# Where the memory rows' softmax sums stand in a segment's attention stretch, and how its spare work is cut

## The chip, the cores and the metric

One core of one Trainium2 chip runs the whole program. The metric is the device time of one execution in microseconds (us). Engines are named as in the profile: PE (matmul), PEld (weight loads of the same engine), DVE (VectorE), ACT (ScalarE), POOL (GpSimd), SP (a DMA queue).

## The reference

Two kinds of layers alternate, A, B, A, B, on x of 2048 tokens by 512. A is attention with a recurrent memory: 64 segments of 32 tokens, in order, and each needs the 8 memory rows that the one before it gave.

```python
for s in range(n_seg):                      # 64 segments, one after the other
    h = concatenate([mem, xs], axis=1)      # 8 memory rows + 32 tokens
    q, k, v = h @ Wq, h @ Wk, h @ Wv        # 32 heads of 128
    scores = where(mask, q @ k.T * scale, -1e9)
    p = softmax(scores)                     # exp, and its row sum
    o = (p @ v) @ Wo
    mem = o[:, :8]; outs.append(o[:, 8:])
```

B is a gated MLP over all tokens (gelu, a 2048x2048 mixing of tokens, a product). The change concerns A alone: two A layers of 64 segments, 128 in all.

## The kernel before, in words

A segment is computed by `segment(s, ...)` inside `a_block`, with all 32 heads at once, in two halves of 16 heads: r = 0 and r = 1. The order of the instructions on PE, DVE and ACT is the order in which they are written (`tc.manual_schedule`); each engine runs its own list in order. The order of one segment on PE is:

1. The projections (L762): q and k of both halves (`psQ`, `psm`, `psK`), and v of half 0 (`psK`), with the scores of half 0 (`psS`, L1113 and L1117) between.
2. Half of v of half 1 (`psV`, L762), the scores of half 1, and the rest of v of half 1. ACT takes the exponentials (`S`, L1122), DVE multiplies them with the mask (`close`, `E`, L1125).
3. The stretch: `pv(0)` and `pv(1)` (L1162, L1165) multiply the exponentials with the values into `psO[0]` and `psO[1]`. Each of the two is a PSUM tile of two banks; columns 0 to 319 of a bank hold these products. The softmax sums come from matmuls with a matrix of ones: `sums_tokens` (L1154, `psT`) for the tokens' rows; for the memory rows `sums_zero` for half 0 (L1136), which writes into free columns of the score tile `psS` and runs among the matmuls of v, and `sums_one` for half 1 (L1145), into columns 320 to 383 of `psO[1]`, between the token sums and `pv(1)`.
4. The memory rows: `inverse(r)` takes 1/sum on ACT as exp(-ln(sum)) (L1179, then L1180, tile `Rm`), `memory_out(r)` on DVE (L1183) multiplies it with the products into `uT`. The output product of half 0 is `px` (`wo_pairs`, L945), that of half 1 `psO<-Wo` (`wo_rest`, L952). Their sum, turned, is the memory of the next segment (`fold`, `build_hA`, `hT`), without which its projections can't begin.

Work that no segment waits for at once is handed out by `fill()`, which advances a generator by one step: the projections of a later block's tokens (`b_units`, `b_even`, `b_light`) or output products of finished tokens (`y_part`). A quarter is one group of four matmuls in four column groups, 512 columns each. `fill()` is called three times in a segment: ahead of `pv(0)`, ahead of `px`, and behind `wo_rest`. In segments fed by `b_units` and `y_part` the three calls give 1, 2 and 5 quarters (full segments); in those fed by `b_even` and `b_light` 1, 1 and, as a rule, 4 (light segments). Light are segments 0 to 15 and 28 to 59 of the first A layer (of them, 0 has its own order) and 0 to 15 of the second.

`close(r)` is followed on the value side by a copy out of PSUM: `VA` of half 0 on DVE (L1211), of half 1 on ACT (L1226, 512 columns), which stands between the two steps of `inverse(0)`:

```python
            invert = inverse(0, pN.rearrange("p (g q) -> p g q", g=2))
            nc.scalar.copy(VA[:, 1].rearrange("p i e -> p (i e)"), psW[:])
            invert()
            close(1)
```

Of the kernel before, what the change touches and what calls it, by code (L numbers as in the profile page):

```python
# [7 lines left out]
BF16 = mybir.dt.bfloat16  # L8
# [6 lines left out]
P = 128  # L15
# [52 lines left out]
def _consts(ctx, tc, c, b_sp, between):  # L68
    nc = tc.nc
    cp = ctx.enter_context(tc.tile_pool(name="consts", bufs=1))  # L70
    bsp = cp.tile([P, 16], F32, name="bsp")
    tctx = ExitStack()
    tmp = tctx.enter_context(tc.tile_pool(name="consts_tmp", bufs=1))
    maskf = tmp.tile([P, 224], F32, name="maskf")
    nc.gpsimd.memset(maskf[:], 1.0)
    fourth = tmp.tile([P, 4, 32], F32, name="fourth")
    nc.gpsimd.memset(fourth[:], 0.0)
    nc.gpsimd.affine_select(out=fourth[:], in_=fourth[:], compare_op=ALU.not_equal, fill=1.0,
                            base=0, pattern=[[-1, 4], [-4, 32]], channel_multiplier=1)
    own = maskf[:, 160:224].rearrange("p (i q) -> p i q", i=4)  # L80
    is_own = tmp.tile([P, 4, 1], F32, name="is_own")
    nc.vector.tensor_reduce(out=is_own[:], in_=fourth[:], op=ALU.max, axis=mybir.AxisListType.X)
    nc.vector.tensor_copy(own, is_own[:].to_broadcast([P, 4, 16]))
    between()
    for q in range(0, P, 32):
        blk = maskf[q:q + 32, 0:160].rearrange("p (i q) -> p i q", i=4)[:, :, 8:32]
        nc.gpsimd.affine_select(out=blk, in_=blk, compare_op=ALU.is_ge, fill=0.0, base=8,
                                pattern=[[0, 4], [1, 24]], channel_multiplier=-1)
        last = own[q:q + 32, :, 8:16]
        nc.gpsimd.affine_select(out=last, in_=last, compare_op=ALU.is_ge, fill=0.0, base=0,  # L90
                                pattern=[[1, 4], [4, 8]], channel_multiplier=-1)
    maskN = cp.tile([P, 2, 224], BF16, name="maskN")
    nc.vector.memset(maskN[:], 0.0)
    for gs in range(4):
        nc.vector.tensor_copy(maskN[32 * gs:32 * gs + 32, gs % 2, :], maskf[32 * gs:32 * gs + 32, :])
    ones = cp.tile([P, P], BF16, name="ones")
    nc.vector.memset(ones[:], 1.0)
    half = cp.tile([P, 2, 32], BF16, name="half")
    nc.vector.memset(half[:], 0.0)
    for g in range(2):  # L100
        nc.vector.memset(half[64 * g:64 * g + 64, g, :], 1.0)
    bsp_bf = cp.tile([P, 16], BF16, name="bsp_bf")

    def load_bsp():
        nc.vector.memset(bsp_bf[:], 0.0)
        nc.sync.dma_start(bsp_bf[:], b_sp.rearrange("(t p) -> p t", p=P))
        return lambda: nc.vector.tensor_copy(bsp[:], bsp_bf[:])

    c["bsp"], c["load_bsp"] = bsp, load_bsp
    tctx.close()  # L110
    c.update(maskN=maskN, ones=ones, half=half)
    return c


# [603 lines left out]
def a_block(tc, c, rows, front, MV_in, RS_in, MV_out, RS_out, ahead, wo, S, first):  # L718
    nc = tc.nc
    NSEG = S // SEG  # L720
    NB = S // P
    scale = float(DH) ** -0.5
    maskN, ones, half = c["maskN"], c["ones"], c["half"]

    with ExitStack() as ctx:

# [38 lines left out]
        def other_bank(mms, *reads):  # L765

            for m in mms:
                for r in reads:
                    tc.declare_no_dep(m.ins, r.ins, reason="another bank of the tile")
# [48 lines left out]
        def b_units(tb, early=0, alone=False):  # L818
            bs = blk_state[tb]
            order = (0, 2, 1, 3, 4, 5) if early else (4, 5, 0, 2, 1, 3)  # L820

            for k, j in enumerate(order):
                now = k < early
                ps = (accB if k % 2 and not alone and not (now and j == 5) else accA).tile([P, 512], F32, name="psb")[:]
                for kts in (((0,), (1, 2), (3,)), ((0, 1, 2, 3),))[k % 2 or alone]:
                    b_mms(bs, j, ps, kts, now)
                    if kts[-1] != KT - 1:
                        yield

                def out(k=k, j=j, ps=ps, now=now):  # L830
                    b_out(bs, k % 2, j, ps, now, j == (5 if alone else 4))

                if now or k % 2 == 0:
                    copies.append(out)
                else:
                    copies.insert(0, out)
                if now or k % 2 or alone:
                    yield
# [164 lines left out]
        def y_part(G, q, last=False):  # L1003

            for k, _ in enumerate(y_steps(G, q, last)):
                if k in (0, 2):
                    yield
            yield

# [60 lines left out]
        def segment(s, fill, spare1, spare2, spare3, tail, loads):  # L1070
# [4 lines left out]
            VA = vsp.tile([P, 2, 4, DH], BF16, name="VA")  # L1075
# [6 lines left out]
            E = segp.tile([P, 2, 2, 224], BF16, name="E", bufs=1)  # L1082
# [9 lines left out]
            def v_mm(r, ps, kts=range(KT)):  # L1092
                return mm_chunk(ps, lambda kt, cg: hA_cur[:, kt, :], lambda kt, cg: cols_rhs(w, 4 + r, kt, cg), kts)
# [30 lines left out]
            def close(r):  # L1124
                nc.vector.tensor_tensor(out=E[:, r], in0=S[:, r].unsqueeze(1).to_broadcast([P, 2, 224]), in1=maskN[:], op=ALU.mult)  # L1125

            def e_all(e, lo, hi):

                return e[:, :, 0:160].rearrange("p n (i q) -> p n i q", q=40)[:, :, :, lo:hi]

            def e_own(e, b):
                return e[:, :, 160:224].rearrange("p n (i b e) -> p n i b e", i=4, b=2)[:, :, :, b, :]

            def sums_zero(pN):

                return [nc.tensor.matmul(pN[32 * cg:32 * cg + 32, 64 * g:64 * g + 64], lhsT=half[:, g, :], rhs=e_own(E[:, 0], 0) if k else e_all(E[:, 0], 0, 8),  # L1136
                                         start=False, stop=True, tile_position=(0, 32 * cg), skip_group_check=True)
                        for k in range(2) for g in range(2) for cg in range(4)]

            def sums_one():  # L1140

                for k in range(2):
                    for g in range(2):
                        e = E[64 * g:64 * g + 64, 1]
                        nc.tensor.matmul(psO[1][:, g, 320:384], lhsT=ones[64 * g:64 * g + 64, :], rhs=e_own(e, 0) if k else e_all(e, 0, 8),  # L1145
                                         start=(k == 0), stop=True, skip_group_check=True)

            def sums_tokens(ps):

# [7 lines left out]
            def pv(r):  # L1157

                for i in range(4):
                    for g in range(2):  # L1160
                        o = psO[r][:, g, 0:320].rearrange("p (s i q) -> p s i q", s=2, i=4)[:, :, i, :]
                        nc.tensor.matmul(o, lhsT=VA[64 * g:64 * g + 64, r, i, :], rhs=E[64 * g:64 * g + 64, r, :, 40 * i:40 * i + 40],  # L1162
                                         start=(r == 0 and i == 0), stop=True, skip_group_check=True)
                for g in range(2):
                    nc.tensor.matmul(ends(heads40(psO[r][:, g, 0:320])), lhsT=VX[64 * g:64 * g + 64, j4, r, :],  # L1165
                                     rhs=E[64 * g:64 * g + 64, r, :, 160:224], start=False, stop=True, skip_group_check=True)
# [10 lines left out]
            def inverse(r, src):  # L1177
                rm = Rm[:, r]
                nc.scalar.activation(out=rm, in_=src, func=ACT.Ln)  # L1179
                return lambda: nc.scalar.activation(out=rm, in_=rm, func=ACT.Exp, scale=-1.0)  # L1180
# [24 lines left out]
            psS = att.tile([P, 2, 512], F32, name="psS")  # L1205
            scores(0)
            expd = exps(0)
# [8 lines left out]
            psW = accB.tile([P, 512], F32, name="psV")  # L1216
            v_mm(1, psW, (0, 1))
            other_bank(scores(1), expd)
            expd = exps(1)
            v_mm(1, psW, (2,))  # L1220
            pN = psS[:, 0, 224:352]
            other_bank(sums_zero(pN), expd)
            v_mm(1, psW, (3,))
            Rm = segp.tile([P, 2, 2, 64], F32, name="Rm", bufs=1)
            invert = inverse(0, pN.rearrange("p (g q) -> p g q", g=2))
            nc.scalar.copy(VA[:, 1].rearrange("p i e -> p (i e)"), psW[:])  # L1226
            invert()
            close(1)

            psO = [attO[r].tile([P, 2, 512], F32, name="psO") for r in range(2)]  # L1230
            if not begin:
                fill()
            pv(0)
            psT = att.tile([P, 2, 512], F32, name="psT")
            sums_tokens(psT)
            sums_one()
            pv(1)
            memory_out(0)
            spare1(E)
            if not begin:  # L1240
                fill()
            inverse(1, psO[1][:, :, 320:384])()
            memory_out(1)
            run(copies)
            Rt = segp.tile([P, 2, 512], F32, name="Rt", tag="Rt", bufs=1)
# [247 lines left out]
```

## Time and profile before

| | us |
|---|---|
| median of three runs | 1604.93 (1603.9 to 1605.56) |
| the profiled execution, its own time | 1610.6 |
| its span in the trace | 1608.9 |
| PE busy | 1579.1 (98%) |
| DVE busy | 1070.4 (67%) |
| ACT busy | 1052.3 (65%) |
| POOL busy | 306.5 (19%) |

Times within the trace are microseconds from the start of the span. A line of the timeline shows the start, the length, the engine, the line of the code, the operation, the tiles (written <- read), how many instructions it takes together, and in brackets how long the engine had been idle and what ended that. A row of matmuls lasts from the first start to the last end. In the chain of waits a piece lasts from the end of the piece before it to its own end.

### The profile page before, as it was taken

The numbers are of one execution on the slowest core, as the hardware profiler recorded it, in microseconds if no ns is written. First come the engines' busy times: TensorE is split into PE (matmuls) and PEld (weight loads), VectorE is DVE, ScalarE is ACT, GpSimd is POOL, SyncE is SP. The second block draws the span as 40 slices with busy tenths as digits, with TensorE's granted clock in tenths as the row PEclk, the third lists the DMA queues.
The fourth block names the chain that finished last, engine by engine and source line by source line (L and its number), as shares of the span: only waits on it lengthen the run. The fifth ranks groups of instructions, "written<-read, shape, count | busy, mean of one in ns | idle before, by whom it ended". The sixth has DMA issues, their size and how long they took to land.

```text
span 1608.9 us, 90911 instructions
## 1 busy us (share of the span) xinstructions
PE 1579.1 (98%) x41021; PEld 981.3 (61%) x41046; DVE 1070.4 (67%) x3066; ACT 1052.3 (65%) x2279; POOL 306.5 (19%) x674
## 2 busy tenths in 40 slices
PE   7899999999999999999999999999999999999999
PEld 3566666666666666666656666666666766665565
DVE  4667766677777776784466666666677667768622
ACT  4677777777777777670057777777777777776400
POOL 6211111112211221320011111111122122224000
PEclk9999999999999999999999999999999999999999
DMA  9322112222311332378952212212233223426698
GB/s 364 131 57 46 40 44 44 50 42 82 80 43 40 87 86 61 106 172 175 209 162 45 48 44 50 44 47 46 73 92 73 47 72 92 97 54 178 143 194 164
DMA packets 255773, 149.67 MB, mean 93 GB/s; under 512 B 188504, under 2 KB 231104, under 8 KB 255384
## 3 DMA queue, kind: packets, MB, share of 16 engines
q1 hardware_dynamic: 241464, 97.68, 27.4%
q0 software_dynamic: 13920, 46.18, 8.9%
q8 instruction: 321, 5.26, 1.4%
q14 instruction: 68, 0.56, 0.1%
HBM read 60.21 MB, written 39.55 MB: 62 GB/s over the span
## 4 chain that ended last, share of the span: by engine, by line
PE 92%; DMA 5%; issue 1%; DVE 1%; ACT 1%; POOL 1%; SPq 0%; POOLq 0%; DVEq 0%; ACTq 0%
PE psQ L762 13%; PE psK L762 13%; PE psb L762 9%; PE pg L403 9%; PE psO L952 7%; PE px L945 7%; PE psm L762 7%; PE psV L762 7%; PE pwB L964 3%; PE psO L1162 3%; PE pz L302 3%; PE py L446 2%; PE psT L1154 2%; PE psS L1113 2%; DMA Wk_sb<-in_A_Wk_dram 1%
## 5 line engine op out<-in xcount | busy, mean ns | idle before, releaser
L762 PEld LDWEIGHTS <-hT 128*32 128x32 bf16 x12288 | 345.3, 96 | 259.2 <-DVE hT L1062 17.7
L762 PE MATMUL psV<-Wv_sb,hT 128*32 128x512 bf16 x2048 | 166.4, 379 | 0.0
L1087 ACT CAST rows<-psQ 128x512 bf16<-128x512 f32 x256 | 145.4, 588 | 23.2 <-PE psQ L762 19.4
L1183 DVE TENSOR_TENSOR uT<-psO,Rm 128x128 bf16<-128x128 f32 x256 | 74.6, 291 | 123.6 <-ACT Rm L1180 123.4
L1090 DVE STREAM_TRANSPOSE QQ<-rows 128x256 f32<-128x256 f32 x256 | 112.5, 439 | 66.2 <-ACT rows L1087 63.6
L1122 ACT ACTIVATE S<-psS 128x224 bf16<-128x224 f32 x256 | 92.2, 360 | 98.1 <-PE psS L1117 98.1
L1090 DVE STREAM_TRANSPOSE KA<-rows 128x256 f32<-128x256 f32 x256 | 113.0, 441 | 64.9 <-ACT rows L1087 62.4
L403 PE MATMUL pg<-z,wspT 128*128 128x344 bf16 x1024 | 154.3, 309 | 0.0
L762 PE MATMUL psK<-Wv_sb,hT 128*32 128x512 bf16 x2048 | 153.2, 378 | 0.0
L1186 DVE TENSOR_TENSOR uT<-psO,Rt 128x384 bf16<-128x384 f32 x256 | 139.9, 547 | 16.4 <-ACT Rt L1265 14.4
L1265 ACT ACTIVATE Rt<-Rt 128x512 f32<-128x512 f32 x256 | 147.3, 622 | 4.0
L952 PE MATMUL psO<-Wo_high,uT 128*32 128x128 bf16 x8192 | 143.0, 219 | 4.1 <-issue 2.2
L762 PE MATMUL psQ<-Wq_sb,hT 128*32 128x512 bf16 x2048 | 136.4, 379 | 0.2 <-issue 0.2
L762 PE MATMUL psQ<-Wk_sb,hT 128*32 128x512 bf16 x2048 | 136.2, 379 | 0.0
L762 PE MATMUL psK<-Wk_sb,hT 128*32 128x512 bf16 x2048 | 136.0, 379 | 0.0
L762 PE MATMUL psm<-Wq_sb,hT 128*32 128x512 bf16 x2048 | 136.0, 379 | 0.0
L945 PE MATMUL px<-Wo,uT 128*32 128x256 bf16 x3840 | 133.8, 273 | 1.3 <-issue 1.2
L952 PEld LDWEIGHTS <-uT 128*32 128x32 bf16 x8192 | 123.6, 97 | 16.2 <-issue 7.8
L403 PEld LDWEIGHTS <-wspT 128*128 128x128 bf16 x1024 | 100.1, 98 | 53.4 <-issue 0.4
L1262 ACT ACTIVATE Rt<-psT 128x1024 f32<-128x1024 f32 x127 | 130.1, 1024 | 3.1
L945 PEld LDWEIGHTS <-uT 128*32 128x32 bf16 x4096 | 104.5, 97 | 25.2 <-issue 2.6
L1044 POOL COPY KX<-old 128x128 bf16<-128x128 bf16 x128 | 65.5, 539 | 263.8 <-PE psS L1117 170.7
(224 smaller groups left out, 2892.9 us busy)
## 6 DMA issues: line engine op xcount, KB each, us to landing
o_d<-o_sb SPq DMA_DIRECT2D x126, 64.0 KB
vb_d<-front SPq DMA_DIRECT2D x31, 256.0 KB
VX<-vb_d SPq DMA_DIRECT2D x124, 64.0 KB
ln_x<-xd SPq DMA_DIRECT2D x26, 256.0 KB
y_o<-o_d POOLq DMA_DIRECT2D x22, 256.0 KB, 3.4
xd<-y_o POOLq DMA_DIRECT2D x22, 256.0 KB, 3.2
Wq_sb<-in_A_Wq_dram POOLq DMA_DIRECT2D x8, 512.0 KB, 7.1
Wk_sb<-in_A_Wk_dram POOLq DMA_DIRECT2D x8, 512.0 KB, 9.3
```

Of the source, the lines that this page charges most:

```text
L403: nc.tensor.matmul(pg[t][:, k, 0:344], lhsT=wsp[t][:, st, :], rhs=z(st, 344 * k, 344 * k + 344), start=(st == 0), stop=(st == NT - 1))
L762: return [nc.tensor.matmul(ps[32 * cg:32 * cg + 32, :], lhsT=lhs(kt, cg), rhs=rhs(kt, cg), start=(kt == 0), stop=(kt == KT - 1), tile_posi ...
L945: nc.tensor.matmul(px[at:at + 32, 0:256], lhsT=lhs[:, h, :], rhs=wo_rhs(h, slice(k + 2, None, -2) if h % 2 else slice(k, None, 2)), start= ...
L952: nc.tensor.matmul(pw[32 * cg:32 * cg + 32, :], lhsT=lhs[:, h, :], rhs=wo_rhs(h, cg), start=False, stop=(h == H - 1), tile_position=(0, 32 ...
L1044: eng.tensor_copy(KX[r][:].rearrange("p g (k i) -> p i g k", i=4), bs["KTB"][:, r].rearrange("p (i g) k -> p i g k", i=4)[:, :, :, 8 * j4: ...
L1087: return r, mms, copy(r[:].rearrange("p (n el two) -> p n el two", n=8, two=2), ps.rearrange("p (n two el) -> p n el two", n=8, two=2))
L1090: nc.vector.transpose(out=(QQ[:, j % 2, :, 0:32] if j < 2 else KA[:, j % 2]).bitcast(F32).rearrange("p n q one -> p n (q one)"), in_=r[:]. ...
L1122: return nc.scalar.activation(out=S[:, r], in_=psS[:, r, 0:224], func=ACT.Exp, scale=scale)
L1183: nc.vector.tensor_tensor(out=hview(uT_cur[:], r, 24, 32), in0=oview(r, 0, 8), in1=Rm[:, r].rearrange("p g (n q) -> p g n q", q=8), op=ALU ...
L1186: nc.vector.tensor_tensor(out=hview(uT_nxt[:], r, 0, 24), in0=oview(r, 8, 32), in1=rview(r, 0, 24), op=ALU.mult)
L1262: nc.scalar.activation(out=Rt[:], in_=psT[:], func=ACT.Ln)
L1265: nc.scalar.activation(out=rt, in_=rt, func=ACT.Exp, scale=-1.0)
```

## The change

- `sums_zero` and the constant `half` go. A new `sums_memory` makes the memory sums of both halves with four matmuls each, as `sums_one` did for half 1.
- The banks are exchanged: the sums of half 0 are put into columns 320 to 383 of `psO[1]`, those of half 1 into the same columns of `psO[0]`.
- The order in the stretch becomes: fill, sums of half 0, `pv(0)`, sums of half 1, token sums, `pv(1)`, `memory_out(0)`, fill, `inverse(1)`, `memory_out(1)`. Both steps of `inverse(0)` are issued behind the sums of half 0.
- The value copy of half 1 is made in two pieces of 256 columns, one on ACT, one on DVE.
- The steps of `b_units` and `y_part` are cut so that the three calls of `fill()` give 2, 1 and 5 quarters in full segments. `b_even` and `b_light` are as they were.

```diff
@@ b_units
-                for kts in (((0,), (1, 2), (3,)), ((0, 1, 2, 3),))[k % 2 or alone]:
+                for kts in (((0, 1), (2,), (3,)), ((0, 1, 2, 3),))[k % 2 or alone]:
@@ y_part
-                if k in (0, 2):
+                if k in (1, 2):
                     yield
@@ segment
-            def sums_zero(pN):
-
-                return [nc.tensor.matmul(pN[32 * cg:32 * cg + 32, 64 * g:64 * g + 64], lhsT=half[:, g, :], rhs=e_own(E[:, 0], 0) if k else e_all(E[:, 0], 0, 8),
-                                         start=False, stop=True, tile_position=(0, 32 * cg), skip_group_check=True)
-                        for k in range(2) for g in range(2) for cg in range(4)]
-
-            def sums_one():
+            def sums_memory(r, ps, begun):
 
                 for k in range(2):
                     for g in range(2):
-                        e = E[64 * g:64 * g + 64, 1]
-                        nc.tensor.matmul(psO[1][:, g, 320:384], lhsT=ones[64 * g:64 * g + 64, :], rhs=e_own(e, 0) if k else e_all(e, 0, 8),
-                                         start=(k == 0), stop=True, skip_group_check=True)
+                        e = E[64 * g:64 * g + 64, r]
+                        nc.tensor.matmul(ps[:, g, :], lhsT=ones[64 * g:64 * g + 64, :], rhs=e_own(e, 0) if k else e_all(e, 0, 8),
+                                         start=(k == 0 and not begun), stop=True, skip_group_check=True)
@@
-            v_mm(1, psW, (2,))
-            pN = psS[:, 0, 224:352]
-            other_bank(sums_zero(pN), expd)
-            v_mm(1, psW, (3,))
+            v_mm(1, psW, (2, 3))
+            close(1)
+            for k, copy in enumerate((nc.scalar.copy, nc.vector.tensor_copy)):
+                copy(VA[:, 1, 2 * k:2 * k + 2].rearrange("p i e -> p (i e)"), psW[:, 256 * k:256 * k + 256])
             Rm = segp.tile([P, 2, 2, 64], F32, name="Rm", bufs=1)
-            invert = inverse(0, pN.rearrange("p (g q) -> p g q", g=2))
-            nc.scalar.copy(VA[:, 1].rearrange("p i e -> p (i e)"), psW[:])
-            invert()
-            close(1)
 
             psO = [attO[r].tile([P, 2, 512], F32, name="psO") for r in range(2)]
             if not begin:
                 fill()
+            sums = [psO[1 - r][:, :, 320:384] for r in range(2)]
+            sums_memory(0, sums[0], False)
+            inverse(0, sums[0])()
             pv(0)
+            sums_memory(1, sums[1], True)
             psT = att.tile([P, 2, 512], F32, name="psT")
             sums_tokens(psT)
-            sums_one()
             pv(1)
             memory_out(0)
             spare1(E)
             if not begin:
                 fill()
-            inverse(1, psO[1][:, :, 320:384])()
+            inverse(1, sums[1])()
             memory_out(1)
```

More of the change, by code (lines that the diff above doesn't have):

```diff
@@ L97, in _consts @@
     nc.vector.memset(ones[:], 1.0)
[L98 to L101, printed above, removed]
     bsp_bf = cp.tile([P, 16], BF16, name="bsp_bf")
@@ L110, in _consts @@
     tctx.close()
-    c.update(maskN=maskN, ones=ones, half=half)
+    c.update(maskN=maskN, ones=ones)
     return c
@@ L722, in a_block @@
     scale = float(DH) ** -0.5
-    maskN, ones, half = c["maskN"], c["ones"], c["half"]
+    maskN, ones = c["maskN"], c["ones"]
     with ExitStack() as ctx:
```

## The prediction

> **What bounds the kernel now.** I read the page first, then the chain of waits over one segment, then the timeline of the same stretch, then the list of waits.
>
> ```profile
> span 1608.9 us, 90911 instructions
> ...
> PE 1579.1 (98%) x41021; PEld 981.3 (61%) x41046; DVE 1070.4 (67%) x3066; ACT 1052.3 (65%) x2279; POOL 306.5 (19%) x674
> ...
> PE 92%; DMA 5%; issue 1%; DVE 1%; ACT 1%; POOL 1%; SPq 0%; POOLq 0%; DVEq 0%; ACTq 0%
> ```
>
> PE is nearly never idle and carries 92% of the chain: now each piece of PE's work costs its own length, and any wait put on PE costs its own length too. The chain of waits through one full segment (segment 25 of the first A layer; start, length, piece):
>
> ```profile
> 295.37 0.22 PE psV L762 x4
> 295.59 0.12 PE psS L1136 x16
> 295.70 0.22 PE psV L762 x4
> 295.92 0.22 PE psb L762 x4
> 296.14 0.25 PE psO L1162 x8
> 296.39 0.06 PE psO L1165 x2
> 296.44 0.30 PE psT L1154 x4
> 296.74 0.06 PE psO L1145 x4
> 296.80 0.14 PE psO L1162 x8
> 296.95 0.06 PE psO L1165 x2
> 297.00 0.55 PE psb L762 x8
> 297.55 0.87 PE px L945 x32
> 298.42 0.89 PE psO L952 x64
> ```
>
> There is PE alone in it, without a gap. A quarter costs 0.22; the first piece behind a change between the column form of the projections and the 64-row form of the stretch has some 0.11 on top (0.25 against 0.14 for the same eight matmuls; 0.55 for two quarters). `sums_zero` costs 0.12, the four-matmul form 0.06. The timeline of the same stretch shows what runs beside it:
>
> ```profile
> 295.12 0.68 DVE L1211 CAST VA<-psK 128x512 bf16<-128x512 f32 x1
> 295.46 0.36 ACT L1122 ACTIVATE S<-psS 128x224 bf16<-128x224 f32 x1 [0.75 <-PE psS L1117]
> 295.85 0.39 DVE L1125 TENSOR_TENSOR E<-S,maskN 128x448 bf16<-128x448 bf16 x1
> 295.97 0.58 ACT L1226 CAST VA<-psV 128x512 bf16<-128x512 f32 x1
> 296.07 0.32 PE L1162 MATMUL psO<-E,VA 64*128 64x80 bf16 x8
> 296.45 0.31 ACT L1180 ACTIVATE Rm<-Rm 128x128 f32<-128x128 f32 x1
> 296.58 0.22 PE L1145 MATMUL psO<-E,ones 64*128 64x64 bf16 x4
> 296.78 0.22 PE L1165 MATMUL psO<-E,VX 64*128 64x128 bf16 x2
> 296.80 0.29 DVE L1183 TENSOR_TENSOR uT<-psO,Rm 128x128 bf16<-128x128 f32 x1 [0.56 <-ACT Rm L1180]
> 297.04 0.28 ACT L1179 ACTIVATE Rm<-psO 128x128 f32<-128x128 f32 x1 [0.28 <-PE psO L1165]
> 297.35 0.31 ACT L1180 ACTIVATE Rm<-Rm 128x128 f32<-128x128 f32 x1
> 297.37 1.04 PE L945 MATMUL px<-Wo,uT 128*32 128x256 bf16 x30
> 297.69 0.29 DVE L1183 TENSOR_TENSOR uT<-psO,Rm 128x128 bf16<-128x128 f32 x1 [0.27 <-ACT Rm L1180]
> 298.25 1.07 PE L952 MATMUL psO<-Wo_high,uT 128*32 128x128 bf16 x64
> ```
>
> I count from S, the start of the second exponential (295.46), since all of the change lies behind it. `memory_out(0)` ends at 296.80 + 0.29, S + 1.63, and `px` starts at S + 1.91; `memory_out(1)` ends at 297.69 + 0.29, S + 2.52, and `wo_rest` (psO L952) starts at S + 2.79. So both memory products are ready some 0.27 before PE needs them: slack, and the change spends it. A light segment (30) shows how much slack there is without the second quarter ahead of `px`:
>
> ```profile
> 345.17 0.36 ACT L1122 ACTIVATE S<-psS 128x224 bf16<-128x224 f32 x1 [0.75 <-PE psS L1117]
> 345.79 0.32 PE L1162 MATMUL psO<-E,VA 64*128 64x80 bf16 x8
> 346.51 0.29 DVE L1183 TENSOR_TENSOR uT<-psO,Rm 128x128 bf16<-128x128 f32 x1 [0.56 <-ACT Rm L1180]
> 346.65 0.40 PE L964 MATMUL pwB<-Wo_high,front 128*32 128x512 bf16 x4
> 346.88 1.04 PE L945 MATMUL px<-Wo,uT 128*32 128x256 bf16 x30
> 347.41 0.29 DVE L1183 TENSOR_TENSOR uT<-psO,Rm 128x128 bf16<-128x128 f32 x1 [0.61 <-ACT Rm L1180]
> 347.76 1.08 PE L952 MATMUL psO<-Wo_high,uT 128*32 128x128 bf16 x64
> ```
>
> None: `memory_out(1)` ends at 347.41 + 0.29 = 347.70, and `wo_rest` starts 0.06 later. That 0.06 is the handoff from DVE to a started matmul. Here `px` starts at S + 1.71, `wo_rest` at S + 2.59.
>
> **The change part by part.**
>
> *The sums of half 0.* Sixteen matmuls (0.12) become four (0.06): PE gains 0.06 a segment. No change of form is added, because the new four stand ahead of `pv(0)` in its form and take over the 0.11 that `pv(0)` pays now. The matrix `half` costs three memsets fewer, once: nothing. But the sums come later. `pv(0)` starts at S + 0.61 in the full segment and at S + 0.62 in the light one. Without the 0.12, and with one more quarter (0.22) in the full segment alone, the new sums start at S + 0.71 and S + 0.50. Four of them last 0.22 (row L1145): they end at S + 0.93 and S + 0.72. ACT begins 0.04 after a matmul's end (296.78 + 0.22 to 297.04).
>
> *From the sums to `px`.* The rows of half 1 give the length of ln, exp and product without a break: 297.04 to 297.98, 0.94. So `memory_out(0)` ends at S + 0.93 + 0.04 + 0.94 = 1.91 (full) and 0.72 + 0.04 + 0.94 = 1.70 (light), and `px` starts 0.06 later: S + 1.97 and S + 1.76. What PE could do: from `pv(0)` to `px` it needs now 1.30 (full: 1.91 - 0.61) and 1.09 (light: 1.71 - 0.62). Behind the change there are 0.06 of sums more and, in the full segment, one quarter less: it is there at S + 0.71 + 1.30 + 0.06 - 0.22 = 1.85, and at S + 0.50 + 1.09 + 0.06 = 1.65. It waits 0.12 and 0.11, and `px` is 0.06 and 0.05 later than now.
>
> *From `memory_out(0)` to `wo_rest`.* Here lies the larger cost. The sums of half 1 are now in `psO[0]`, which `memory_out(0)` reads on DVE. In the list of waits ln of half 1 now waits for `pv(1)`:
>
> ```profile
> ACT Rm L1179 <- PE psO L1165: 38.8, 128, 1.9
> ```
>
> Its own sums (296.58 + 0.22 = 296.80) were ready 0.24 before it started; it waited for the last other instruction on the same tile, 128 times of 128. So a reader of `psO` is ordered behind what stands before it on that tile, whichever columns those touch. In the instructions of the changed kernel, in their built order, ln of half 1 carries one wait, on DVE, for `memory_out(0)` of its own segment; the wait for `pv(1)` is gone from it. The Trainium skill ("PSUM — Partial Sum Buffer", section on bank collisions) says that two engines may not touch one bank and quadrant at once, "reads against reads included", and that PSUM is guarded by bank and not by address: by that rule this wait has to be there. Without it the sum would be that of the second rival below. The price of the wait: from DVE's end to ACT's start it is 0.03 (741.29 + 0.18 to 741.50):
>
> ```profile
> 741.29 0.18 DVE L146 BATCH_NORM_AGGREGATE MV<-bnst 128x2 f32<-128x6 f32 x1
> 741.50 0.29 ACT L122 ACTIVATE RS<-MV,eps_t 128x1 f32<-128x1 f32 x1 [19.33 <-DVE MV L146]
> ```
>
> So ln of half 1 starts at S + 1.94 and 1.73, `memory_out(1)` ends 0.94 later, S + 2.88 and 2.67, and `wo_rest` starts 0.06 later: S + 2.94 and S + 2.73. Now they are 2.79 and 2.59. That is 0.15 and 0.14 a segment. Queued behind the waiting ln on ACT are exp, the copies that are due and the `cross` copy of `px`, which ends later than ln and exp anyway; behind `memory_out(1)` on DVE is the fold, which waits for `px` in any case.
>
> *The value copy in two pieces.* Not in the trace. ACT takes 0.28 for 128 columns (L1179) and 0.58 for 512, so some 0.38 for 256; DVE 0.29 (L1183) and 0.68 (L1211), so some 0.42. psV is ready 0.12 earlier: ACT's piece runs from S + 0.39 to 0.77, ln of half 0 in the light segment (S + 0.76) just about fits. In the built order DVE's piece waits for ACT's, so it runs from S + 0.80 to 1.22, and the second half of `pv(1)` may start at S + 1.28. PE is there at S + 0.71 + 0.06 + 0.20 + 0.06 + 0.30 + 0.07 = 1.40 (full) and 1.19 (light): 0.09 of waiting, which the 0.11 before `px` swallows. I take nothing for it. At the lower bound, 0.28 and 0.29, that also holds; at the upper, 0.58 and 0.68, PE comes late to `px` by about 0.2 in every segment: the third rival. `pv(1)` also waits for ln of half 0 (S + 0.97 + 0.28, full), and the second sums for `close(1)` (S + 0.78): both within 0.1 of PE's own time and under the same cover.
>
> *The quarters.* In full segments one quarter moves from between `pv(1)` and `px` to ahead of the sums, without which the sums would be 0.22 sooner, but PE 0.22 nearer to `px` too. It is paid for already above. Behind `wo_rest` five stay, so the way from `wo_rest` over the fold and the turned memory to the next projections is as it is.
>
> *Sum.* 64 full segments at 0.15 and 63 light ones at 0.14 (segment 0 of the first layer is bound by loads and left out): 9.6 + 8.8 = 18.4 us, on the profiled execution's own 1610.6: 1629.0. The median lies 5.7 below that execution, and I carry that over: 1604.9 + 18.4 = 1623.3. Put otherwise: PE saves 0.06 and gets 0.12 of waiting before `px` and 0.1 before `wo_rest`. Error of the steps: 0.03 on the four handoffs and the start after a wait makes 4 to 5 us either way, so 1618 to 1629.
>
> **The rivals.**
>
> *Work sets the end (faster).* If ln, exp and product came through in time, PE's 0.06 less would be all: 127 x 0.06 = 7.6, 1597.3. For that `memory_out(0)` has to end at S + 1.79 in place of 1.91, and ln of half 1 must not be held by it. For it speaks PE's share of the chain, against it that all three durations repeat in both segments shown. Chance 0.06.
>
> *One wait only.* If ln of half 1 is not held by `memory_out(0)`, `wo_rest` follows `px` directly (0.88 behind it, as now): 0.06 and 0.05 a segment, 7.0 us, 1612. The row of L1179 speaks against it. Chance 0.08. Between this and the first rival lies what can't be told from no change (0.2%, 3.2 us).
>
> *The copies bind.* If the halved copies take nearly what the whole ones take, `pv(1)` is late and with it `px`: about 0.2 in each of 127 segments on top where they are at the upper bound, 25 us, 1649; halfway, 1636. It decides from the point where DVE's piece ends after S + 1.25 in light and 1.35 in full segments. Chance 0.11.
>
> **How the numbers follow.** Forecast 1623, chance 0.75, own range 1618 to 1629. For 8 in 10 the range reaches down to the second rival's side, 1613, and up toward the third, 1632. Slower by over 0.2% are the forecast, the third rival and most of the second: 0.91; faster 0.06; within 0.2% 0.03.
>
> **What would show it.** In the changed profile: ln of half 1 idle until DVE's `memory_out(0)`, in nearly all 128 segments; PE's weight loads of `px` and of `wo_rest` waiting for `uT`; `px` at about S + 1.97 and S + 1.76, `wo_rest` 0.97 behind it; PE busy less by some 0.2 a segment while the span grows. I am wrong if `wo_rest` follows `px` at 0.88, if `px` starts before S + 1.91 in full segments, or if `pv(1)` waits for the copies so long that `px` is late by it.

## The result and the profile after

The changed kernel took 1621.85 us (median of 4 runs, 1618.62 to 1622.56), the kernel before 1604.74 (median of 4, 1603.9 to 1605.56) beside it: ratio 1.0103, 95% interval 1.0089 to 1.0118. It is slower by 17.1 us. The forecast was 1623.0, range 1613 to 1632. The two profiled executions lie only 8.0 us apart (spans 1608.9 and 1616.9); why the medians differ more is taken up at the end.

The page of the changed kernel, span and busy times:

```profile
span 1616.9 us, 87837 instructions
...
PE 1595.1 (99%) x39510; PEld 944.1 (58%) x39510; DVE 1126.3 (70%) x3191; ACT 1050.7 (65%) x2279; POOL 305.6 (19%) x674
```

PE is busy for 16.0 us more, though the page counts 1511 matmuls fewer. The forecast had it less busy. Half of the 16.0 us is the longer span (8.0 us), the other half idle time of PE, which shrank from 29.8 to 21.8 us. A look at one segment says why a PE that waits counts as busy. The timeline of full segment 98 of the changed kernel (counted through both A layers, so segment 34 of the second; lines are shifted: ln is L1169, exp L1170, `memory_out` L1173, `px` L941, `wo_rest` L948, the value copy L1213, the memory sums L1135; S is 1172.43):

```profile
1172.43 0.36 ACT L1118 ACTIVATE S<-psS 128x224 bf16<-128x224 f32 x1 [0.75 <-PE psS L1113]
...
1172.82 0.37 ACT L1213 CAST VA<-psV 128x256 bf16<-128x256 f32 x1
...
1173.13 0.23 PE L1135 MATMUL psO<-E,ones 64*128 64x64 bf16 x4
...
1173.22 0.42 DVE L1213 CAST VA<-psV 128x256 bf16<-128x256 f32 x1
...
1173.41 0.28 ACT L1169 ACTIVATE Rm<-psO 128x128 f32<-128x128 f32 x1 [0.21 <-PE psO L1135]
...
1174.06 0.29 DVE L1173 TENSOR_TENSOR uT<-psO,Rm 128x128 bf16<-128x128 f32 x1 [0.41 <-ACT Rm L1170]
...
1174.38 0.28 ACT L1169 ACTIVATE Rm<-psO 128x128 f32<-128x128 f32 x1 [0.36 <-DVE uT L1173]
1174.40 0.78 PEld L941 LDWEIGHTS <-uT 128*32 128x32 bf16 x32 [0.26 <-DVE uT L1173]
...
1175.03 0.29 DVE L1173 TENSOR_TENSOR uT<-psO,Rm 128x128 bf16<-128x128 f32 x1 [0.35 <-ACT Rm L1170]
...
1175.38 0.68 PEld L948 LDWEIGHTS <-uT 128*32 128x32 bf16 x48 [0.20 <-DVE uT L1173]
```

Read the brackets downward. ln of half 0 begins 0.05 after its sums (1173.13 + 0.23). `memory_out(0)` ends at 1174.35; ACT, idle for 0.36, is released by it (`<-DVE uT L1173`) and begins ln of half 1 at 1174.38; the weight loads of `px` are released by the same product at 1174.40. `memory_out(1)` ends at 1175.32 and releases `wo_rest` at 1175.38. So `px` stands at S + 1.97 and `wo_rest` 0.98 behind it.

A light segment (30) of the changed kernel, S = 346.35, with the fold of `px` (tile `t`) and the first quarter behind `wo_rest`:

```profile
346.35 0.36 ACT L1118 ACTIVATE S<-psS 128x224 bf16<-128x224 f32 x1 [0.75 <-PE psS L1113]
...
348.10 0.28 ACT L1169 ACTIVATE Rm<-psO 128x128 f32<-128x128 f32 x1 [0.36 <-DVE uT L1173]
...
348.12 1.05 PE L941 MATMUL px<-Wo,uT 128*32 128x256 bf16 x30
...
349.09 0.90 PEld L948 LDWEIGHTS <-uT 128*32 128x32 bf16 x64 [0.20 <-DVE uT L1173]
...
349.61 0.29 DVE L1051 TENSOR_TENSOR t<-px,cross 128x128 f32<-128x128 f32 x1
...
350.00 0.39 PE L758 MATMUL psb<-Wq_sb,hB 128*32 128x512 bf16 x4
```

`px` at S + 1.77, `wo_rest` 0.97 behind it, again through DVE's product. The last two rows are for later: the quarter begins 0.91 behind `wo_rest`.

The list of waits of the changed kernel says that these two segments stand for all (engine, line and what it waited for; us in total, times, longest):

```profile
ACT Rm L1169 <- DVE uT L1173: 47.6, 128, 2.0
...
PEld L948 <- DVE uT L1173: 24.3, 122, 0.2
...
PEld L941 <- DVE uT L1173: 18.9, 79, 0.3
```

ln of half 1 waits for `memory_out(0)` 128 times of 128, and the weight loads of both output products wait for `uT` (`px` 79 times, `wo_rest` 122 times), 43.2 us together. That is idle time of the weight loads, not loss of the same size: in segment 98 those of `wo_rest` idle for 0.20, and `wo_rest` is 0.10 later against `px` than before. In the trace of before, the weight loads of `px` waited 0.7 us for `uT` in all. These waits stand on the rows of the weight loads, not of the matmuls: a matmul's row runs on to its modelled end, which covers a wait of 0.1, so PE's busy time grows although its work shrinks. In the segments that simply repeat, PE's rows show no gap in either kernel (worked out from the traces).

### The profile page after: what moved, and what is told of

It reads as the page before. It is cut to its first block, busy times and chain, and to the rows that moved or that the text cites. A ratio compares the mean times of both kernels' runs of the same rounds, so it can differ in the third digit from the quotient of the medians.

```text
span 1616.9 us, 87837 instructions
## 1 busy us (share of the span) xinstructions
PE 1595.1 (99%) x39510; PEld 944.1 (58%) x39510; DVE 1126.3 (70%) x3191; ACT 1050.7 (65%) x2279; POOL 305.6 (19%) x674
## 4 chain that ended last, share of the span: by engine, by line
PE 93%; DMA 3%; DVE 1%; issue 1%; ACT 1%; POOL 0%; POOLq 0%; SPq 0%; DVEq 0%; ACTq 0%
PE psQ L758 13%; PE psK L758 13%; PE psb L758 10%; PE pg L399 9%; PE px L941 8%; PE psO L948 8%; PE psm L758 7%; PE psV L758 7%; PE pwB L960 3%; PE pz L298 3%; PE py L442 2%; PE psO L1152 2%; PE psT L1144 2%; PE psO L1135 2%; PE psS L1109 2%
## 5 line engine op out<-in xcount | busy, mean ns | idle before, releaser
L758 PEld LDWEIGHTS <-hT 128*32 128x32 bf16 x12288 | 315.1, 97 | 274.5 <-DVE hT L1058 22.0
L758 PE MATMUL psV<-Wv_sb,hT 128*32 128x512 bf16 x2048 | 150.3, 378 | 0.0
L1176 DVE TENSOR_TENSOR uT<-psO,Rt 128x384 bf16<-128x384 f32 x256 | 140.2, 548 | 10.9 <-ACT Rt L1254 1.2
L1173 DVE TENSOR_TENSOR uT<-psO,Rm 128x128 bf16<-128x128 f32 x256 | 74.7, 292 | 98.1 <-ACT Rm L1170 96.8
L948 PE MATMUL psO<-Wo_high,uT 128*32 128x128 bf16 x8192 | 139.3, 220 | 0.5 <-issue 0.3
L941 PE MATMUL px<-Wo,uT 128*32 128x256 bf16 x3840 | 135.5, 275 | 0.4 <-issue 0.3
L948 PEld LDWEIGHTS <-uT 128*32 128x32 bf16 x8192 | 116.5, 97 | 26.3 <-DVE uT L1173 24.3
L941 PEld LDWEIGHTS <-uT 128*32 128x32 bf16 x4096 | 99.2, 97 | 28.2 <-DVE uT L1173 18.9
```

The lines of the kernel that those rows point to most:

```text
L758: return [nc.tensor.matmul(ps[32 * cg:32 * cg + 32, :], lhsT=lhs(kt, cg), rhs=rhs(kt, cg), start=(kt == 0), stop=(kt == KT - 1), tile_posi ...
L941: nc.tensor.matmul(px[at:at + 32, 0:256], lhsT=lhs[:, h, :], rhs=wo_rhs(h, slice(k + 2, None, -2) if h % 2 else slice(k, None, 2)), start= ...
L948: nc.tensor.matmul(pw[32 * cg:32 * cg + 32, :], lhsT=lhs[:, h, :], rhs=wo_rhs(h, cg), start=False, stop=(h == H - 1), tile_position=(0, 32 ...
L1173: nc.vector.tensor_tensor(out=hview(uT_cur[:], r, 24, 32), in0=oview(r, 0, 8), in1=Rm[:, r].rearrange("p g (n q) -> p g n q", q=8), op=ALU ...
L1176: nc.vector.tensor_tensor(out=hview(uT_nxt[:], r, 0, 24), in0=oview(r, 8, 32), in1=rview(r, 0, 24), op=ALU.mult)
```

## Experiments

Each ratio is to the kernel before on the same chip. Periods (start of the `psQ` projections to the next such start, in segments without a stall) are worked out from the traces: before 10.03 in full and 9.67 in light segments, changed 10.21 and 9.78. That is 64 x 0.18 + 63 x 0.11 = 18.4 us. Not every segment repeats so. Some take longer than the rest of their kind, which is called a stall here: of the 62 full and 63 light periods within the two layers, 32 and 30 lie within 0.03 of the given figure before, and 52 and 33 in the changed kernel. Nearly all others are longer; they are taken up at e11.

**e1, e3: the sums back in one bank pair.** Both sums go into `psO[1]`, side by side; e3 also puts the quarters back (the edit of e2).

```diff
-            sums = [psO[1 - r][:, :, 320:384] for r in range(2)]
+            sums = [psO[1][:, :, 320 + 64 * r:384 + 64 * r] for r in range(2)]
...
-            pw = psO[1][:, 0, 384:512]
+            pw = psO[0][:, 0, 384:512]
```

> The changed kernel, but the sums of half 1 go into columns 384 to 447 of psO[1], beside those of half 0, and the output product psO<-Wo into psO[0]. In the built order ln of half 1 then waits for pv(1) on PE and no longer for memory_out(0) on DVE. Theory A (two waits: the first puts px 0.06 later, the second, ln of half 1 behind memory_out(0), puts wo_rest another 0.10 later): the second goes, wo_rest follows px at 0.87 to 0.88 in place of 0.976, px stays at S + 1.98 and S + 1.765; 0.06 a segment remain against before, 1612 us (1610 to 1614). Theory B (the bank costs nothing; the two-piece copy, the later sums and the order of the quarters cost all of it): 1622 as the changed kernel.

> Both edits together: sums of half 1 in psO[1], quarters 1, 2 and 5. Theory A: full segments as with the quarters alone (px at S + 1.94, wo_rest 0.88 behind it), light segments as with the bank alone (px S + 1.765, wo_rest 0.88 behind it): 0.03 a full and 0.05 a light segment over before, 1610 us (1607 to 1612). Theory B: 1622 or more.

Measured: e1 1637.52 us, 1.0165 [1.0146, 1.0185]; e3 1636.84 us, 1.0161 [1.0142, 1.0179]. In e1 both theories missed. e3 is slow, as theory B said, but for a cause that neither theory names. e1, full segment 98:

```profile
1184.73 0.36 ACT L1118 ACTIVATE S<-psS 128x224 bf16<-128x224 f32 x1 [0.75 <-PE psS L1113]
...
1185.71 0.28 ACT L1169 ACTIVATE Rm<-psO 128x128 f32<-128x128 f32 x1 [0.21 <-PE psO L1135]
...
1186.04 0.23 PE L1135 MATMUL psO<-E,ones 64*128 64x64 bf16 x4 [0.17 <-ACT Rm L1169]
...
1186.90 1.04 PE L941 MATMUL px<-Wo,uT 128*32 128x256 bf16 x30
...
1187.77 0.46 PE L948 MATMUL psO<-Wo_high,uT 128*32 128x128 bf16 x20
```

The wait for `memory_out(0)` is gone, as expected: `wo_rest` is 0.87 behind `px`. But `px` is at S + 2.17. The sums of half 1 (1186.04) now write the tile that ln of half 0 is reading (1185.71 + 0.28 = 1185.99), in other columns, and they wait for it. That is PE itself, and all behind it is late. The list of waits of e1:

```profile
PE psO L1135 <- ACT Rm L1169: 21.3, 124, 0.2
```

124 times (e3: 126 times, 21.7 us). The exchange thus has a use: with the sums of half 1 ahead of the token sums, one bank pair would cost more than the exchange does.

**e6: one bank pair, the sums of half 1 behind the token sums.** The second edit lets ln of half 0 end before PE gets to the sums.

```diff
-            sums = [psO[1 - r][:, :, 320:384] for r in range(2)]
+            sums = [psO[1][:, :, 320 + 64 * r:384 + 64 * r] for r in range(2)]
...
-            sums_memory(1, sums[1], True)
             psT = att.tile([P, 2, 512], F32, name="psT")
             sums_tokens(psT)
+            sums_memory(1, sums[1], True)
...
-            pw = psO[1][:, 0, 384:512]
+            pw = psO[0][:, 0, 384:512]
```

> The changed kernel with the sums of half 1 in psO[1] beside those of half 0 (the product psO<-Wo in psO[0]), and these sums made behind the token sums. In the run with the bank alone PE itself waited, because the sums of half 1 write the tile that ln of half 0 is reading; behind the token sums that ln has just ended. Theory A: px stays at S + 1.98 and S + 1.765, wo_rest follows at 0.873 in place of 0.976: 0.063 a full and 0.055 a light segment over before, 7.5 us, ratio 1.0047. Theory B (the bank costs nothing): 1.0103 or more.

Measured: 1612.29 us, 1.0022 [1.0007, 1.0037]. Full segment 98 of e6:

```profile
1170.43 0.36 ACT L1118 ACTIVATE S<-psS 128x224 bf16<-128x224 f32 x1 [0.75 <-PE psS L1113]
...
1172.22 0.28 ACT L1169 ACTIVATE Rm<-psO 128x128 f32<-128x128 f32 x1 [0.18 <-PE psO L1155]
...
1172.42 1.05 PE L941 MATMUL px<-Wo,uT 128*32 128x256 bf16 x30
...
1173.30 0.62 PE L948 MATMUL psO<-Wo_high,uT 128*32 128x128 bf16 x32
```

ln of half 1 is released by `pv(1)` (L1155), no longer by DVE; `px` is at S + 1.99 and `wo_rest` 0.88 behind it. The first wait is all that is left: periods 10.11 and 9.75. This is the state that the rival "One wait only" described. So in the changed kernel the exchange of banks costs 0.10 a full and 0.03 a light segment, and the other 0.08 arises ahead of `px`. By its segments e6 should lose 127 x 0.08 = 10.2 us, and it lost 3.2 (interval 1.1 to 6.0); e1, by 10.30 and 9.93, should lose 33.7 and lost 25.8. What takes back 7 to 8 us is not in the segments without a stall; I come back to it at e11.

**e5: the exchange alone, in the kernel before.** The sums of half 1 go into `psO[0]`, where they stood otherwise.

```diff
-                        nc.tensor.matmul(psO[1][:, g, 320:384], lhsT=ones[64 * g:64 * g + 64, :], rhs=e_own(e, 0) if k else e_all(e, 0, 8),
-                                         start=(k == 0), stop=True, skip_group_check=True)
+                        nc.tensor.matmul(psO[0][:, g, 320:384], lhsT=ones[64 * g:64 * g + 64, :], rhs=e_own(e, 0) if k else e_all(e, 0, 8),
+                                         start=False, stop=True, skip_group_check=True)
...
-                                         start=(r == 0 and i == 0), stop=True, skip_group_check=True)
+                                         start=(i == 0), stop=True, skip_group_check=True)
...
-            inverse(1, psO[1][:, :, 320:384])()
+            inverse(1, psO[0][:, :, 320:384])()
```

> The kernel before with the exchange of banks alone: the sums of half 1 go to columns 320 to 383 of psO[0], those of half 0 stay early, in the score tile; in the built order ln of half 1 then waits for memory_out(0). Theory A (the wait costs only what exceeds the slack): ln of half 1 moves from S + 1.585 to S + 1.66 and memory_out(1) ends at S + 2.60; full segments have slack to S + 2.73 and lose nothing, light ones lose 0.08 before wo_rest and get about half of it back behind it, where they now wait 0.04 for the fold: 1 to 3 us, ratio 1.0012. Theory B (the exchange costs 0.1 in every segment): 12 us, ratio 1.008.

Measured: 1619.38 us, 1.0072 [1.0049, 1.0094]. Full segments keep 10.03, as theory A said; light ones lose 0.15, which it did not (63 x 0.15 = 9.4 us; measured 10.3). Light segment 30 of e5:

```profile
346.70 0.36 ACT L1122 ACTIVATE S<-psS 128x224 bf16<-128x224 f32 x1 [0.75 <-PE psS L1117]
...
347.82 0.22 PE L1145 MATMUL psO<-E,ones 64*128 64x64 bf16 x4
...
348.16 0.29 DVE L1183 TENSOR_TENSOR uT<-psO,Rm 128x128 bf16<-128x128 f32 x1 [0.68 <-PE psO L1145]
...
348.50 1.05 PE L945 MATMUL px<-Wo,uT 128*32 128x256 bf16 x30
```

`memory_out(0)` itself now waits for the sums of half 1 (347.82 + 0.22 = 348.04), the last to write its tile, and begins at S + 1.46, where it began at 1.34 before (346.51 - 345.17). `px` is 0.09 later (S + 1.80 against 1.71), and ln of half 1 is chained behind it too. Full segments have the second quarter as cover.

**e2: the quarters as before (1, 2, 5) in the changed kernel. e8: the quarters alone (2, 1, 5) in the kernel before.** The edit of e2; e8 is its reverse.

```diff
-                for kts in (((0, 1), (2,), (3,)), ((0, 1, 2, 3),))[k % 2 or alone]:
+                for kts in (((0,), (1, 2), (3,)), ((0, 1, 2, 3),))[k % 2 or alone]:
...
-                if k in (1, 2):
+                if k in (0, 2):
```

> The changed kernel with the steps of b_units and y_part as before the change: 1, 2 and 5 quarters in full segments; light segments unchanged. Theory A: the sums of full segments come 0.22 sooner, so px is no longer held by memory_out(0) but by PE's own work, at about S + 1.94; ln of half 1 ends early enough and wo_rest follows px at 0.88, S + 2.82 in place of 2.95. 0.14 less in each of 64 full segments: 1613 us (1611 to 1616); light segments as in the changed kernel. Theory B (the quarter ahead of the stretch covers the late copy and is needed): pv(1) waits for the copy, px is at S + 2.0 or later, 1622 or more.

> The kernel before with the quarters of full segments at 2, 1 and 5, and nothing else. Theory A: the sums of half 0 stay early, so px is where it was (S + 1.91); pv(1) and with it ln of half 1 are 0.22 later, memory_out(1) ends at S + 2.74 and wo_rest starts at S + 2.80, 0.01 later than before: 0 to 1 us, ratio 1.0005. If the quarter ahead of the stretch costs by itself what the changed kernel showed for it (0.13 in each full segment): 8 us, ratio 1.005.

Measured: e2 1616.72 us, 1.0035 [1.0021, 1.0048]; e8 1610.31 us, 1.0013 [0.9998, 1.0028]. Full segment 98 of e2:

```profile
1169.83 0.36 ACT L1118 ACTIVATE S<-psS 128x224 bf16<-128x224 f32 x1 [0.75 <-PE psS L1113]
...
1170.22 0.39 DVE L1121 TENSOR_TENSOR E<-S,maskN 128x448 bf16<-128x448 bf16 x1
...
1170.63 0.42 DVE L1213 CAST VA<-psV 128x256 bf16<-128x256 f32 x1
1170.66 0.23 PE L1135 MATMUL psO<-E,ones 64*128 64x64 bf16 x4
...
1170.99 0.36 PE L1152 MATMUL psO<-E,VA 64*128 64x80 bf16 x8
...
1171.78 1.04 PE L941 MATMUL px<-Wo,uT 128*32 128x256 bf16 x30
...
1172.66 0.68 PE L948 MATMUL psO<-Wo_high,uT 128*32 128x128 bf16 x36
```

Full segment 98 of e8:

```profile
1161.31 0.36 ACT L1122 ACTIVATE S<-psS 128x224 bf16<-128x224 f32 x1 [0.75 <-PE psS L1117]
...
1163.19 1.04 PE L945 MATMUL px<-Wo,uT 128*32 128x256 bf16 x30
```

In e8 `px` is at S + 1.88, no later than before, and nothing is lost: early sums in `psS` do not mind a quarter behind them. In e2 `px` is at S + 1.95 and `wo_rest` 0.88 behind it, so PE waits for neither product; full segments take 10.07, light ones 9.78 as in the changed kernel. The quarter ahead costs 0.14 a full segment, but only together with the late sums.

10.07 is still 0.04 more than before, though PE has less to do. The rows show two smaller waits that the quarter had covered: the sums of half 1 begin 0.05 after the mask product of half 1 has ended (1170.22 + 0.39 to 1170.66), and `pv(1)` takes 0.36, where segment 98 of the changed kernel has 0.32; it needs DVE's piece of the copy, which ends at 1171.05. In the chain of waits of this segment the four sums take 0.14 in place of 0.06, and the eight matmuls of `pv(1)` 0.18 in place of 0.14. Theory B of e2 was thus right in kind, but not in size.

**e10: one bank pair, the order of e6, the quarters of e2.**

> The changed kernel with three things at once: both memory sums in the second bank pair, those of half 1 behind the token sums, and the quarters as before (1, 2, 5). Theory A (two waits, one of which the quarter ahead of the sums makes in full segments): neither wait is left in full segments: px where PE arrives, S + 1.95 as with the quarters put back, wo_rest 0.88 behind, period 10.07; light segments as with that order alone, 9.75. By the segments 64 x 0.04 + 63 x 0.08 = 7.6 us, ratio 1.0047; since the last two kernels of this kind measured 2 to 4 thousandths under the sum of their segments, down to 1.001. Rival B (the loss hangs on the new form and place of the sums as such, not on the waits): 1.008 or more.

Measured: 1618.03 us, 1.0038 [1.0022, 1.0054]. Full segment 98 of e10:

```profile
1170.17 0.36 ACT L1118 ACTIVATE S<-psS 128x224 bf16<-128x224 f32 x1 [0.75 <-PE psS L1113]
...
1172.13 1.04 PE L941 MATMUL px<-Wo,uT 128*32 128x256 bf16 x30
...
1173.00 1.07 PE L948 MATMUL psO<-Wo_high,uT 128*32 128x128 bf16 x64
```

`px` at S + 1.96, `wo_rest` 0.87 behind: neither of the two waits in full segments, which repeat in 10.07, as theory A said. Light ones repeat in 9.75. By the segments that is 64 x 0.04 + 63 x 0.08 = 7.6 us; measured 6.2, interval 3.5 to 8.7. With these quarters the exchange costs a full segment nothing: e2 has it, e10 has not, and both take 10.07. So the costs of the parts can't simply be added up. The late sums were not run by themselves in the kernel before; e10 comes nearest to that, and still has the two pieces of the copy.

**e4: no sums in the memory product.** DVE multiplies the memory rows with a constant in place of `Rm`; PE's and ACT's work stays.

```diff
-                nc.vector.tensor_tensor(out=hview(uT_cur[:], r, 24, 32), in0=oview(r, 0, 8), in1=Rm[:, r].rearrange("p g (n q) -> p g n q", q=8), op=ALU.mult)
+                nc.vector.tensor_scalar(out=hview(uT_cur[:], r, 24, 32), in0=oview(r, 0, 8), scalar1=0.025, scalar2=None, op0=ALU.mult)
```

> The changed kernel with memory_out(r) multiplying by the constant 0.025 in place of the inverse sums, so the memory rows are not normalised by their own sums; ln and exp run as before and nobody waits for their results. It shows what PE's own work would take. Theory A: px follows the quarter ahead of it without a wait (about 0.13 sooner in full, 0.04 in light segments), wo_rest follows px at 0.87: 0.06 to 0.07 less than before in full segments and about 0.01 more in light ones, 1601 us (1597 to 1605). Theory B (work, copies and forms cost it): 1615 or more.

Measured: 1608.62 us, 0.9986 [0.9973, 0.9998]. Full segment 98 of e4:

```profile
1164.88 0.36 ACT L1118 ACTIVATE S<-psS 128x224 bf16<-128x224 f32 x1 [0.75 <-PE psS L1113]
...
1166.73 1.04 PE L941 MATMUL px<-Wo,uT 128*32 128x256 bf16 x30
```

Without the chain `px` starts at S + 1.85, where the prediction had PE arrive (1.85). In light segments it starts at 1.74 (worked out from the trace), not at 1.65, and the period is 9.71. The prediction had 0.09 of waiting inside the stretch there, for the copy (1.28 against 1.19), and let the wait ahead of `px` cover it; 1.65 + 0.09 is the 1.74 that shows when the cover is gone. The rows say that the mask product and the copy share it: in segment 30 of e4 the sums of half 1 take 0.14 of the chain of waits and the eight matmuls of `pv(1)` 0.18, as in e2. So 0.04 of the 0.11 that a light segment loses does not hang on ln, exp and product.

**e7: the value copy in one piece. e9: the two pieces alone, in the kernel before.**

```diff
-            for k, copy in enumerate((nc.scalar.copy, nc.vector.tensor_copy)):
-                copy(VA[:, 1, 2 * k:2 * k + 2].rearrange("p i e -> p (i e)"), psW[:, 256 * k:256 * k + 256])
+            nc.scalar.copy(VA[:, 1].rearrange("p i e -> p (i e)"), psW[:])
```

```diff
-            nc.scalar.copy(VA[:, 1].rearrange("p i e -> p (i e)"), psW[:])
+            nc.scalar.copy(VA[:, 1, :2].rearrange("p i e -> p (i e)"), psW[:, :256])
             invert()
             close(1)
+            nc.vector.tensor_copy(VA[:, 1, 2:].rearrange("p i e -> p (i e)"), psW[:, 256:])
```

> The changed kernel with the value copy of half 1 in one piece on ACT, as before. Theory A: pv(1) gets its values sooner, which doesn't matter; in light segments ln of half 0 stands behind the longer copy, S + 0.90 in place of 0.77, and px is 0.13 later; full segments as in the changed kernel: 8 us more than the changed kernel, ratio 1.015. Theory C (the two-piece copy binds the changed kernel): less than the changed kernel, ratio 1.005.

> The kernel before with one part of the change alone: the value copy of half 1 in two pieces of 256 columns, ACT's between the two steps of the inverse of half 0, DVE's behind the second mask product. Theory A (the copies have cover and are no term of the sum): full segments keep their period of 10.03, px at S + 1.91, wo_rest 0.88 behind; light segments have little room, for DVE's piece ends at S + 1.25 and the second half's value product needs it at S + 1.25: 0 to 0.05 a light segment; ratio to the kernel before 1.000 to 1.002. Rival C (the copies are part of the loss): px late by 0.1 in every segment, ratio 1.008.

Measured: e7 1629.25 us, 1.0127 [1.0107, 1.0147]; e9 1626.79 us, 1.0094 [1.0065, 1.0124]. Light segment 30 of e7:

```profile
350.24 0.36 ACT L1118 ACTIVATE S<-psS 128x224 bf16<-128x224 f32 x1 [0.75 <-PE psS L1113]
...
351.12 0.28 ACT L1169 ACTIVATE Rm<-psO 128x128 f32<-128x128 f32 x1
...
352.12 1.05 PE L941 MATMUL px<-Wo,uT 128*32 128x256 bf16 x30
```

With one piece ln of half 0 begins at S + 0.88 (in the changed kernel 0.77, from its trace) and `px` at 1.88 in place of 1.77: in light segments the halves save 0.11. Full ones are as in the changed kernel. So the rival "The copies bind", with its 0.2 in every segment, falls there. In e9 it is the other way round. Full segment 98 of e9:

```profile
1170.13 0.36 ACT L1122 ACTIVATE S<-psS 128x224 bf16<-128x224 f32 x1 [0.75 <-PE psS L1117]
...
1170.64 0.37 ACT L1226 CAST VA<-psV 128x256 bf16<-128x256 f32 x1
...
1171.05 0.42 DVE L1229 CAST VA<-psV 128x256 bf16<-128x256 f32 x1
...
1171.31 0.47 PE L1162 MATMUL psO<-E,VA 64*128 64x80 bf16 x8
...
1172.20 1.04 PE L945 MATMUL px<-Wo,uT 128*32 128x256 bf16 x30
```

Here ACT takes ln of half 0 first and its piece ends at S + 0.88; DVE's piece waits for that and ends at S + 1.34, and `pv(1)` (1171.31) is stretched to 0.47, where the same eight matmuls of `pv(0)` took 0.32. `px` is at S + 2.07, 0.16 later than before, and no wait ahead of `px` swallows it. My expectation had left out that the two pieces run one after the other. In the changed kernel ACT's piece stands ahead of ln and starts at S + 0.39.

**e11: the changed kernel again, on the chip of e9 and e10.**

> The changed kernel as it is, on the same chip as the two others, so that ratios that came from different chips can be set side by side. If ratios carry over between chips: 1.009 to 1.012. If the second wait's share was partly the chip's: below 1.008.

Measured: 1622.48 us, 1.0071 [1.0046, 1.0096], against 1611.79 for the kernel before. The changed kernel came out within 0.6 us of its first measurement, the kernel before 7.1 us above its own. Its periods are those of the first trace, so the second wait is the same. The ratios differ because of the kernel before: on the chips of e1 to e4 and of e5 to e8 it took 1611.74 and 1609.10 us, too, against 1604.74 beside the first measurement of the changed kernel.

The sums by segments miss as well. For e1, e2, e3, e6, e7, e9 and e11 they lie 4 to 8 us above the measured loss; for e4, e5, e8 and e10 they agree within 2 us. The traces say where to look, for the segments with a stall count too. Over all 125 periods, the time beyond the repeating ones adds up to 20 us in the trace of before, 8 in that of the changed kernel and 10 in that of e11 (worked out from the traces). So the 125 periods of the first two differ by 5.4 us in sum, and not by 18. In full segments it is 2.4 to 4.9 us in the seven traces in which PE waits in every one of them, for `uT`, for ln or, in e9, for the copy (changed, e1, e3, e6, e7, e9, e11), and 5.6 to 10.9 us in the six others; in light segments the two groups overlap. So it seems that stalls which PE has without any wait are in part hidden where it waits anyway. That is a pattern over one trace of each kernel; what the stalls are, and why they are fewer there, is not shown. The row that offers itself, the weight loads of `wo_rest` held by nothing that the profile shows (`<- issue`), does not settle it: it reads 7.8 us before and 1.1 in the changed kernel, but 2.5 in e11, the same kernel, and 4.3 both in e7, which has both waits, and in e4, which has neither. Nor is it shown why the loss was 17.1 us on one chip and 10.7 on the other.

## Why the prediction was right

- *The first wait.* Forecast `px` at S + 1.97 and 1.76; measured 1.97 and 1.77. The chain sums, ln, exp, product had been read from half 1 of the old trace and repeats to 0.01. e6 shows this wait by itself (10.11), e4 shows PE at S + 1.85 without it. In light segments PE itself comes at 1.74 and not at the 1.65 that it was given (e4), so of the waiting there 0.09 lies inside the stretch and only 0.03 at `px`.
- *The second wait.* Forecast `wo_rest` 0.97 behind `px`; measured 0.98 and 0.97. e6 takes only its cause away, and `wo_rest` returns to 0.88. The rule that the argument leaned on, in the Trainium skill ("PSUM — Partial Sum Buffer", section "PSUM bank collisions raise a hardware error"), that PSUM is guarded by bank and not by address, agrees: the 124 waits of e1 are a write held by a read of other columns. These are waits that the built program holds, and ln and the products read both banks of their tile, so whether bank or tile decides can't be told here.
- *The copies.* Estimated 0.38 and 0.42, measured 0.37 and 0.42. That they have cover holds in the full segments of the changed kernel, which e7 leaves as they were. It is nearly used up in light ones (e4), falls short without the quarter ahead (e2), and is missing in the kernel before (e9: 0.16 a segment). In light segments they even save 0.11 of ACT's time ahead of ln (e7), which the forecast held implicitly, since it let ln begin at S + 0.76.
- *The quarters.* "Paid already" holds: nothing by themselves (e8), 0.14 a full segment together with the late sums (e2). That does not come on top of the two waits: in full segments the quarter is what makes them.
- *Where it failed.* The step "the way from `wo_rest` to the next projections is as it is" is wrong in light segments. The timeline of before, light segment 30:

```profile
348.36 0.29 DVE L1055 TENSOR_TENSOR t<-px,cross 128x128 f32<-128x128 f32 x1
...
348.71 1.05 PE L762 MATMUL psb<-Wq_sb,hB 128*32 128x512 bf16 x16
```

The first quarter behind `wo_rest` began 0.06 after the fold of `px` had ended (348.65), 0.95 behind `wo_rest` (347.76). In the changed kernel the fold ends at 349.90, and the quarter begins 0.91 behind `wo_rest`: with `wo_rest` later against `px`, the fold no longer holds it. That refunds 0.04; so a light segment costs 0.11, not 0.14. A full one costs 0.18, not 0.15: `wo_rest` starts 0.10 later against `px` (forecast 0.09), 0.01 is lost behind it, and the rest is rounding. The two errors nearly cancel: 18.4 us again, by luck.
- *PE's busy time* was to fall by 0.2 a segment. It rose by 16.0 us: the short waits are inside the rows, and PE's idle time shrank by 8.0 us.
- *From the profiled execution to the median.* On its own scale the forecast was 1629.0, and the changed kernel's profiled execution took 1618.62. The carried-over 5.7 us does not describe the changed kernel, whose profiled execution was the fastest of its four. The stalls of single segments were no term of the sum. On the first chip the loss was 17.1 us, near the 18.4 of the sum; on the later one 10.7. So the 18.4 us is shown for segments that repeat; how much of it reaches the median depends on stalls that the prediction left out. That the measured time lies 1 us from the forecast is in part luck: by an estimate, 1621.85 less the 1609.10 to 1611.79 of the kernel before on the later chips, the loss would have been 10 to 13 us.

No kernel tried here was faster than the one before: e8 can't be told from it, and e4 leaves work out.

## What to carry to other kernels

Before a short sum is moved nearer to its use in order to save matmuls, lay its chain (handoff, ln, exp, product, handoff) against the work that is left between the two places: here 0.06 of work was saved, and 0.12 and 0.10 of waiting bought. Putting data of half A into the tile of half B ties every reader and writer of the two together, even in other columns; list them in each engine's order, and move the order and the place together (e1 and e6 differ in the order alone). A part of a change that costs nothing by itself (e8) or saves something (e7) may be dear beside another (e2, e9): take the parts out one by one, and in both directions.

## What the runs showed of the hardware

- A write of PE into free columns of a `psO` tile waited for ACT's read of other columns, 124 times, 21.3 us (e1). It is a wait of the built program; what would happen without it, no run shows.
- ACT to DVE on one PSUM tile: DVE's piece begins 0.03 to 0.04 after ACT's ends (1172.82 + 0.37 to 1173.22; e9: 1170.64 + 0.37 to 1171.05).
- PE's busy time does not show waits of 0.1: `wo_rest` starts 0.10 later against `px` in the changed kernel, and PE's busy time rose to 1595.1 us of a span of 1616.9. The waits stand on the weight loads (idle 43.2 us for `uT`).
